# Experts, passes two and three: the second product by Strassen's scheme as well, with its operands turned round and a written-out order

## The chip, the cores and the metric

One core of a Trainium2 chip. The metric is the device time of one execution in microseconds (us): 1692.89 us is the median of three runs of the kernel before (1692.16 to 1692.99). The engines are PE (TensorE: matmuls; PEld is its loading of weights), DVE (VectorE), ACT (ScalarE), POOL (GpSimd) and SP, which here only issues DMA transfers.

## The reference, cut to what matters

Causal attention with decay gives `x`, 2304 tokens by 512. The mixture of experts then computes, with `P` a 2304 x 8 gate matrix made by eight rounds of row and column scaling:

```
for e in range(E):                      # E = 8
    h = np.maximum(x @ w1[e], 0.0)      # 512 -> 1024
    ye = h @ w2[e]                      # 1024 -> 512
    out += P[:, e:e + 1] * ye
```

The change is in this loop. The gate values are exponentials times positive scalings, so they are positive.

## The kernel before, in words

Attention runs first, in an order that a planner in the kernel (`arrange`) lays out from a table of durations; it fills the first 240 us or so. The experts follow in three passes of 768 tokens each (two halves of `HT` = 384). In a pass, a unit is one expert `e` and one block `fb` of 256 of its 1024 hidden features: 32 units in a pass, of which two of the first pass are done during attention. Every fp32 operand is split into a high part and a low part (`hi`, `lo`), and each matrix product is three matmuls: hi*hi, hi*lo, lo*hi.

The first product of a unit (`first_fast`, matmuls on L1201) uses Strassen's scheme: seven products of sums of quarter matrices in place of eight. A product is 6 matmuls of 384 columns, so a unit has 42. Its weight sums (S1 to S4) are formed and split in every pass anew, on POOL and ACT (`weight_sums`, `split_sums`); the token sums (T1 to T4) once per pass. DVE adds the seven products up (L1207), ACT and DVE make the high and low part of the relu (`hh` L857, `hl` L860).

The second product (`second`, `combine`, matmuls on L871) is plain: 6 tiles of 128 tokens, each 6 matmuls of 512 columns, 36 in a unit. DVE multiplies each result by the gate value and adds it to `acc` (L1249). A unit's second product stands on PE behind the first product of the unit after it. The last unit of a pass sends `acc` out.

In the expert part each engine works through its queue in the order of the code, except for SP, whose place for a transfer is decided by the framework; an SP transfer that waits holds back those behind it. Two buffers hold raw halves of w1 (`rw`), two of w2 (`rq`). A half is 256 KB.

## Time and profile before

| what | value |
|---|---|
| median of three runs | 1692.89 us |
| span of the profiled execution | 1696.4 us |
| PE busy in the span | 1689.7 us |
| DVE / POOL / ACT busy | 1335.6 / 1120.9 / 682.9 us |
| moved by DMA | 133.11 MB |
| granted TensorE clock, mean | 1.000 |

The profiled execution's own time is its span, 3.5 us above the median of the runs. Busy time of PE is from the start of a matmul to its modelled end; matmuls overlap, so what one costs is read from the distance between starts.

### The profile page before, as it was taken

What the parts mean: (1) busy time and instruction counts of PE and PEld (TensorE: products, weight loads), DVE (VectorE), ACT (ScalarE), POOL (GpSimd) and SP (SyncE); (2) the same over time, 40 slices, a digit from 0 to 9 for tenths busy, and PEclk for the clock granted to TensorE, in tenths of its full rate; (3) what the DMA queues carried; (4) which work ended last, traced back from release to release, by engine and by line L of the source; (5) the groups of instructions that cost most, each with busy time, mean ns of one, the idle gap of its engine ahead of it and who ended that gap; (6) DMA issues with size and microseconds to landing.
All of it is one profiled execution on the core that took longest, in us unless ns stands there. A gap on an engine that the chain in (4) does not pass through costs nothing. (4 is left out here: it accounts for less than half of the span.)

```text
span 1696.4 us, 26313 instructions
## 1 busy us (share of the span) xinstructions
PE 1689.7 (100%) x9179; PEld 1506.5 (89%) x9179; DVE 1335.6 (79%) x2273; ACT 682.9 (40%) x1445; POOL 1120.9 (66%) x1092
## 2 busy tenths in 40 slices
PE   9999999999999999999999999999999999999999
PEld 7888898989898998999899989998998999899988
DVE  6888869888778777777787788777777877787786
ACT  6877743433333333333333333333333333333332
POOL 4556375677766798766666666798766666666663
PEclk9999999999999999999999999999999999999999
DMA  5656312222222222322222222222322222222221
GB/s 133 162 143 161 96 53 69 69 64 74 69 67 65 69 72 63 109 69 69 62 75 70 69 63 69 75 62 63 112 70 64 73 69 69 63 74 71 69 63 62
DMA packets 147098, 133.11 MB, mean 78 GB/s; under 512 B 67371, under 2 KB 116886, under 8 KB 146966
## 3 DMA queue, kind: packets, MB, share of 16 engines
q1 hardware_dynamic: 146966, 131.44, 26.7%
q8 instruction: 72, 1.18, 0.3%
q14 instruction: 60, 0.49, 0.1%
HBM read 126.48 MB, written 4.92 MB: 77 GB/s over the span
## 5 line engine op out<-in xcount | busy, mean ns | idle before, releaser
L871 PE MATMUL po<-early_w,hh 128*128 128x512 f32 x2308 | 715.0, 391 | 1.8 <-DVE acc L1249 1.4
L871 PEld LDWEIGHTS po<-early_w,hh 128*128 128x128 f32 x2308 | 429.1, 188 | 90.2 <-DVE acc L1249 4.1
L1207 DVE TENSOR_TENSOR u<-ph,u 128x384 f32<-128x384 f32 x637 | 344.3, 553 | 205.2 <-PE ph L1201 196.1
L871 PE MATMUL po<-early_w,hl 128*128 128x512 f32 x1154 | 450.6, 391 | 0.0
L1146 POOL TENSOR_TENSOR early_w<-w,early_w 128x512 fp32r<-128x512 f32 x184 | 234.8, 1298 | 306.2 <-ACT early_w L1145 305.4
L860 DVE SCALAR_TENSOR_TENSOR hl<-u,hh 128x384 fp32r<-128x384 f32 x364 | 427.6, 1175 | 12.0 <-ACT hh L857 11.9
L1249 DVE SCALAR_TENSOR_TENSOR acc<-po,prob,acc 128x512 f32<-128x512 f32 x517 | 369.0, 741 | 80.8 <-PE po L871 80.8
L1145 ACT CAST early_w<-w 128x512 fp32r<-128x512 f32 x194 | 120.7, 622 | 553.7 <-issue 535.0
L857 ACT ACTIVATE hh<-u 128x384 fp32r<-128x384 f32 x364 | 190.0, 523 | 320.5 <-DVE u L1207 320.3
L1201 PE MATMUL ph<-t,early_w 128*128 128x384 f32 x1638 | 298.5, 334 | 0.0
L1167 POOL TENSOR_TENSOR early_w<-ws,early_w 128x1024 fp32r<-128x1024 f32 x91 | 222.4, 2444 | 110.4 <-ACT early_w L1164 109.3
L1201 PEld LDWEIGHTS ph<-t,early_w 128*128 128x128 f32 x1638 | 286.0, 188 | 0.0
L871 PEld LDWEIGHTS po<-early_w,hl 128*128 128x128 f32 x1154 | 216.6, 188 | 45.4
L1201 PE MATMUL ph<-xhi,wa 128*128 128x384 f32 x728 | 216.1, 337 | 0.0
L1168 POOL TENSOR_TENSOR wa<-w,wa 128x512 fp32r<-128x512 f32 x91 | 145.5, 1599 | 0.0
L1201 PEld LDWEIGHTS ph<-xhi,wa 128*128 128x128 f32 x728 | 134.1, 188 | 3.5
L1201 PE MATMUL ph<-xlo,wa 128*128 128x384 f32 x364 | 122.3, 336 | 0.0
L1201 PE MATMUL ph<-t,wa 128*128 128x384 f32 x546 | 109.3, 334 | 0.0
L1201 PE MATMUL ph<-xhi,early_w 128*128 128x384 f32 x364 | 107.0, 334 | 0.0
L1164 ACT CAST early_w<-ws 128x1024 fp32r<-128x1024 f32 x91 | 95.8, 1053 | 13.4 <-POOL ws L1157 9.6
L1201 PEld LDWEIGHTS ph<-t,wa 128*128 128x128 f32 x546 | 95.9, 188 | 0.0
L579 ACT ACTIVATE e<-e,mn 128x128 f32<-128x128 f32 (+3 forms) x128 | 70.6, 554 | 12.2 <-DVE mn L572 12.1
(149 smaller groups left out, 1844.8 us busy)
## 6 DMA issues: line engine op xcount, KB each, us to landing
w<-in_moe_w_dram SPq DMA_DIRECT2D x384, 256.0 KB
dn<-cum_d SPq DMA_DIRECT2D x14, 576.0 KB
out_dram<-acc SPq DMA_DIRECT2D x17, 256.0 KB
q<-in_q_dram SPq DMA_DIRECT2D x32, 128.0 KB
k<-in_k_dram SPq DMA_DIRECT2D x32, 128.0 KB
v<-in_v_dram SPq DMA_DIRECT2D x32, 128.0 KB
rb<-r SPq DMA_DIRECT2D x22, 128.0 KB
rz<-in_q_dram SPq DMA_DIRECT2D x32, 16.0 KB
```

The source lines that it names most:

```text
L579: nc.scalar.activation(out=t, in_=t, func=AF.Exp, scale=-1.0, bias=mn[at][:, 0:1], accum_out=place(ss, "ss")[:, at:at + 1],)
L857: nc.scalar.activation(out=hh[:, 0:w], in_=ph[:, 0:w], func=AF.Relu)
L860: nc.vector.scalar_tensor_tensor(out=hl[:, 0:w], in0=ph[:, 0:w], scalar=0.0, in1=hh[:, 0:w].bitcast(F32), op0=ALU.max, op1=ALU.subtract)
L871: nc.tensor.matmul(po[:, cols], ht[:, ts], wt[:, ft, cols], start=(ft == 0 and n == 0), stop=(ft == FB - 1 and n == 2))
L1145: nc.scalar.copy(out=hi[:, s], in_=r)
L1146: a = lo_on.tensor_tensor(out=lo[:, s], in0=r, in1=hi[:, s].bitcast(F32), op=ALU.subtract)
L1164: nc.scalar.copy(out=wsum[0], in_=t)
L1167: nc.gpsimd.tensor_tensor(out=wsum[1], in0=t, in1=wsum[0].bitcast(F32), op=ALU.subtract)
L1168: nc.gpsimd.tensor_tensor(out=lo[:, 1:3], in0=k1, in1=hi[:, 1:3].bitcast(F32), op=ALU.subtract)
L1201: nc.tensor.matmul(ps, ws[y][:, c], xs[z], start=(c == 0 and m == 0), stop=(c == KH - 1 and m == 2))
L1207: nc.vector.tensor_tensor(out=out, in0=in0, in1=in1, op=ALU.add)
L1249: nc.vector.scalar_tensor_tensor(out=to, in0=po[:, cols], scalar=prob[:, t, e:e + 1], in1=to, op0=ALU.mult, op1=ALU.add)
```

## The change

- **Pass one** stays, but each unit's seven weight combinations (high and low) are also written to DRAM (`keep_w1`), for the 27 units that have them there; the gate values of the other two passes are turned and stored (`spread_weights`).
- **Passes two and three** are new. Units are taken in pairs, (e, fb) and (e, fb+1). The seven products of the first scheme (`hidden_product`) read their weights from DRAM, 256 KB each; three of them add in place in one PSUM bank. The result is multiplied by the gate row in the same DVE instruction as the relu (`weigh_relu`), so that the second product can be summed over all experts.
- **The second product** (`out_product`) uses the same scheme, transposed: w2's seven combinations are stationary, the seven combinations of h move, 384 columns at a time. One accumulation takes both units of a pair: 6 matmuls. DVE adds it to one of seven sums M1 to M7 (L1761). Only at the end of a pass are the M's combined (`final_sums`, 7 additions of 768), turned back by PE transposes (`final_turn`) and stored.
- w2's sums and splits (`prepare_w2`), the splits of seven h operands in place of four, and the weight sums of the five units that pass one lacks (`prepare_w1`), with the token sums of pass three kept in DRAM (`prepare_x`), are new work for DVE, POOL and ACT.
- **Order:** the planner lays all this out. PE's order is fixed by the code: for a pair, the products 1, 7, 6, 2, 5, 3, 4 of both units, with the second products 1, 6, 7, 5, 3, 2, 4 of the pair before it between them. The planner's clocks start at PE 16, DVE 12, ACT 10, POOL 10, SP 2 us.

The core of the diff:

```diff
+    def keep_w1(e, fb):
+        d = w1_d[e, fb] = dram.tile([len(COMBOS), P, 2, KH * P], F32, name=f"w1d{e}{fb}")
+        for x in range(2):
+            for ts, a, z in ((wa, 0, 3), (wsum, 3, 7)):
+                nc.sync.dma_start(
+                    out=d[a:z, :, x].rearrange("s p f -> p s f"),
+                    in_=ts[x].rearrange("p s k f -> p s (k f)").bitcast(F32),
+                )
...
                 split_sums(r1, ws)
+                keep_w1(*work[m + 1][1:3])
...
     second(*late)
+    pctx.close()
...
+        "b": [banks[t] for t in ("M0", "M1", "A4", "A5", "A0", "A1")],
+        "s": [banks[t] for t in ("A2", "A3")],
+        "w": w_own + w_acc + from_h,
...
+        if which == "1":
+            keep("u1", X0, X, s)
+        elif which == "7":
+            keep("u7", X2, X, s)
+        elif which == "2":
+            op("c11", X1, X1, t["u1"], ALU.add, ["F2", "u1"], [X, bs["u1"]])
+            weigh_relu("H11", X1, X1, 0, [u.s["c11"]], [X])
+            split("H11", X1, [u.s["H11"]], [X], True)
+        elif which == "6":
+            new("u3")
+            op("u3", t["u3"], X0, t["u7"], ALU.add, ["F6", "u7"], [X, bs["u7"], bs["u3"]])
+        elif which == "5":
+            op("c22", X2, X0, t["u7"], ALU.add, ["F5", "u7"], [X, u.X[2], bs["u7"]])
...
+    moving = {"1": "H11", "3": "H22", "7": "T3", "5": "T1", "6": "T2", "2": "H21", "4": "T4"}
+
+    def out_product(us, which, M, begun, added):
...
+        for k in range(2):
+            b = Buffer("s")
...
+                for (h, _h), (w, _w) in zip(hs, ws):
+                    for y, z in ((0, 0), (0, 1), (1, 0)):
+                        nc.tensor.matmul(
+                            at_(b)[:, 0:HT], at_(w)[y][:, k * P:(k + 1) * P], at_(h)[:, z], start=(i == 0), stop=(i == 5)
+                        )
+                        i += 1
+            s = fpe(6 * pe(HT), run, after=[x for _, d in hs + ws for x in d], uses=[b] + [x for x, _ in hs + ws])
...
+                if begun:
+                    nc.vector.tensor_tensor(out=to, in0=at_(b)[:, 0:HT], in1=to, op=ALU.add)
+                else:
+                    nc.vector.tensor_copy(to, at_(b)[:, 0:HT])
...
+    arranged = arrange(fsteps, slots2, {"PE": 16.0, "DVE": 12.0, "ACT": 10.0, "POOL": 10.0, "SP": 2.0}, 250.0, True)
+    with tc.manual_schedule():
+        for s in arranged:
+            s.run(s.engine)
```

**Where pass one ends.** Before, SP has only the raw halves of w1 and w2 here, unit after unit:

```order
L842 DMA w<-in_moe_w_dram 128x2x256 x2
L842 DMA w<-in_moe_w_dram 128x512 x2
L842 DMA w<-in_moe_w_dram 128x2x256 x2
L842 DMA w<-in_moe_w_dram 128x512 x2
```

Now SP has, from the last stores of `acc` that a pass makes, the first eight weight combinations (`wn`), the gate rows (`pb`) and only then the first raw halves of w2 (`w_8854`, `w_8855`):

```order
L1261 DMA out_0_dram<-acc4_85 128x512
L1626 DMA wn0_8811<-w1d70_8109 128x512
L1261 DMA out_0_dram<-acc5_86 128x512
L1626 DMA wn1_8812<-w1d71_8261 128x512
L1626 DMA wn_8838<-w1d70_8109 128x512
L1626 DMA wn_8839<-w1d71_8261 128x512
L1626 DMA wn_8830<-w1d70_8109 128x512
L1626 DMA wn_8831<-w1d71_8261 128x512
L1626 DMA wn_8832<-w1d70_8109 128x512
L1626 DMA wn_8833<-w1d71_8261 128x512
L1616 DMA pb_8822<-p_d_89 128x768
L850 DMA w_8854<-in_moe_w2_dram 128x512
```

The first load of a combination, `wn0`, goes into memory that the last second product of pass one reads. Behind it, ACT's queue stands like this (L1674 copies product 1 of a unit, from bank M0 and then M1, out of PSUM):

```order
L1156 CAST early_w10_110<-w_8621 128x512
L1448 CAST w2n0_8813<-w_8854 128x256
L1674 COPY u_8850<-bankM0_8842 128x384
L1448 CAST w2n1_8814<-fourw_8841 128x256
L1674 COPY u_8851<-bankM1_8843 128x384
```

The copy of product 1 stands behind the cast of a raw half of w2, and that of the second unit behind a sum of both halves (`fourw`). PE's fifth and sixth products add into M0 and M1 and need these copies.

**In the middle of a pass.** Before, DVE's queue for a unit reads:

```order
L1207 TENSOR_TENSOR u<-ph,u 128x384 x5
L860 SCALAR_TENSOR_TENSOR hl_4249<-u,hh_4248 128x384
L1207 TENSOR_TENSOR u<-ph,u 128x384
L860 SCALAR_TENSOR_TENSOR hl<-u,hh 128x384
L1207 TENSOR_TENSOR u<-ph,u 128x384
L860 SCALAR_TENSOR_TENSOR hl_4245<-u,hh_4244 128x384
L1249 SCALAR_TENSOR_TENSOR acc_83<-po,prob,acc_83 128x512
```

Now it reads, in pass three, behind product 3 of a pair's two units (in banks A0 and A1):

```order
L1679 SCALAR_TENSOR_TENSOR tn_8837<-bankA0_8846,pb_8822 128x384
L1459 TENSOR_TENSOR tn_8834<-tn_8837,bankM0_8842 128x384
L1679 SCALAR_TENSOR_TENSOR u_8853<-bankA1_8847,pb_8822 128x384
L1459 TENSOR_TENSOR u_8852<-bankA4_8844,tn_8834 128x384
L1459 TENSOR_TENSOR u_8851<-u_8853,bankM1_8843 128x384
L1761 TENSOR_TENSOR sum3_8826<-bankA3_8849,sum3_8826 128x384
L1459 TENSOR_TENSOR tn_8835<-bankA5_8845,u_8851 128x384
L1761 TENSOR_TENSOR sum3_8826<-bankA2_8848,sum3_8826 128x384
L1459 TENSOR_TENSOR tn_8834<-bankA4_8844,tn_8837 128x384
```

Nearly every row has one operand in PSUM (`bank`); there are 48 rows for a pair.

**Where pass two's result is turned back, and at the end.** PE's queue at the end of the program (L1752 are second products, L1790 transposes), where there was nothing but the plain second product of the last unit before:

```order
L1790 MATMUL bankA3_8849<-ident_75,sum2_8825 128x128 x2
L1790 MATMUL bankA3_8849<-ident_75,sum4_8827 128x128 x2
L1790 MATMUL bankA2_8848<-ident_75,sum2_8825 128x128 x2
L1790 MATMUL bankA2_8848<-ident_75,sum4_8827 128x128 x2
L1752 MATMUL bankA2_8848<-xlo_80,w2n3_8816 128x384 x3
L1752 MATMUL bankA2_8848<-xhi_79,early_w20_112 128x384 x2
L1752 MATMUL bankA2_8848<-xhi_79,early_w21_113 128x384
L1752 MATMUL bankA2_8848<-xlo_80,w2n3_8816 128x384 x3
L1790 MATMUL bankA3_8849<-ident_75,sum1_8824 128x128 x2
L1790 MATMUL bankA2_8848<-ident_75,sum3_8826 128x128 x2
```

Transposes and second products share the two banks A2 and A3, and the last second product has both its halves in A2.

## Rows read from the trace of the kernel before

**Rows 1.** The page: busy time, share of the span, number of instructions.

```profile
PE 1689.7 (100%) x9179; PEld 1506.5 (89%) x9179; DVE 1335.6 (79%) x2273; ACT 682.9 (40%) x1445; POOL 1120.9 (66%) x1092
```

**Rows 2.** Stretches: PE, PEld, DVE, ACT, POOL busy; clock, DMA share, GB/s.

```profile
0.00:240.00 240.00, 238.41 (x1888) 194.14 (x1889) 187.34 (x626) 169.22 (x501) 126.77 (x209) 1.00 0.50 130
560.00:1660.00 1100.00, 1099.75 (x5530) 996.21 (x5530) 862.54 (x1205) 388.53 (x715) 768.09 (x687) 1.00 0.24 71
```

**Rows 3.** PE in order of time, one unit: start, length.

```profile
1404.76 0.33 PE L1201 MATMUL ph<-xhi,wa 128*128 128x384 f32 x1
...
1412.06 0.63 PE L871 MATMUL po<-early_w,hh 128*128 128x512 f32 x2
...
1420.26 0.33 PE L1201 MATMUL ph<-xhi,wa 128*128 128x384 f32 x1
```

**Rows 4.** DVE, one unit in order of time.

```profile
1409.14 1.60 DVE L1207 TENSOR_TENSOR u<-ph,u 128x384 f32<-128x384 f32 x3 [0.48 <-PE ph L1201]
...
1411.98 0.54 DVE L860 SCALAR_TENSOR_TENSOR hl<-u,hh 128x384 fp32r<-128x384 f32 x1
...
1412.91 2.29 DVE L860 SCALAR_TENSOR_TENSOR hl<-u,hh 128x384 fp32r<-128x384 f32 x1
```

**Rows 5.** POOL in the same unit.

```profile
1412.34 2.45 POOL L1167 TENSOR_TENSOR early_w<-ws,early_w 128x1024 fp32r<-128x1024 f32 x1 [1.17 <-ACT early_w L1164]
```

**Rows 6.** Groups from 1000 to 1660 us: count, busy us, mean ns.

```profile
L1207 DVE TENSOR_TENSOR u<-ph,u 128x384 f32<-128x384 f32 x300 | 162.3, 553 | 100.2 <-PE ph L1201 98.2 <-ACT u L1211 1.3
L1154 POOL TENSOR_TENSOR ws<-w 128x256 f32<-128x256 f32 x43 | 31.7, 738 | 0.0
L1112 POOL TENSOR_TENSOR ts<-xhi,ts 128x384 f32<-128x384 f32 x2 | 2.0, 1020 | 0.2
L857 ACT ACTIVATE hh<-u 128x384 fp32r<-128x384 f32 x170 | 88.8, 523 | 153.8 <-DVE u L1207 153.8
L1145 ACT CAST early_w<-w 128x512 fp32r<-128x512 f32 x86 | 53.5, 622 | 262.5 <-issue 260.0
L1211 ACT COPY u<-ph 128x384 f32<-128x384 f32 x43 | 20.3, 473 | 0.0
L1163 ACT CAST wa<-w 128x256 fp32r<-128x256 f32 x43 | 17.5, 407 | 11.2 <-PE ph L1201 11.2
```

**Rows 7.** POOL in pass one, in order of time.

```profile
483.12 1.60 POOL L1168 TENSOR_TENSOR wa<-w,wa 128x512 fp32r<-128x512 f32 x1
...
492.10 0.74 POOL L1155 TENSOR_TENSOR ws<-w 128x256 f32<-128x256 f32 x1
...
498.62 1.62 POOL L1168 TENSOR_TENSOR wa<-w,wa 128x512 fp32r<-128x512 f32 x1
```

**Rows 8.** Stretches in which one half of w1, released at 484.7, arrives.

```profile
484.50:485.50 1.00, 1.00 (x6) 0.81 (x6) 1.00 (x2) 0.00 (x0) 0.23 (x1) 1.00 0.00 0
485.50:486.50 1.00, 1.00 (x6) 0.84 (x5) 1.00 (x3) 0.00 (x0) 0.00 (x0) 1.00 0.55 119
486.50:487.50 1.00, 1.00 (x7) 0.81 (x5) 0.65 (x2) 0.00 (x0) 0.00 (x0) 1.00 0.42 143
```

**Rows 9.** DMA from 1198 to 1208, GB/s in 40 slices of 0.25 us.

```profile
GB/s 0 0 0 0 0 0 0 0 0 94 98 205 242 369 418 377 328 402 401 410 401 393 410 401 402 402 369 164 8 0 16 106 90 98 213 360 402 401 352 287
```

**Rows 10.** PE where pass two begins, and PE and DVE at the end.

```profile
690.83 0.33 PE L1201 MATMUL ph<-xhi,wa 128*128 128x384 f32 x1
...
706.34 0.33 PE L1201 MATMUL ph<-xhi,wa 128*128 128x384 f32 x1
...
1692.12 0.51 PE L871 MATMUL po<-early_w,hh 128*128 128x256 f32 x2 [0.58 <-DVE acc L1249]
...
1693.14 0.48 DVE L1249 SCALAR_TENSOR_TENSOR acc<-po,prob,acc 128x256 f32<-128x256 f32 x1 [1.07 <-PE po L871]
```

**Rows 11.** PE transposes in the attention part.

```profile
200.24 0.49 PE L715 MATMUL pt<-ident,e 128*128 128x128 f32 x3
```

More of the change, by code (lines that the diff above doesn't have):

```diff
@@ L1305, in attention_then_moe @@
         hts = hts_of[m % 2]
-        if m + 1 < len(work) and work[m + 1][4]:
+        if not last and fast_next:
             ws = weight_sums(r1)
@@ new lines, in loads, with psum_op, lock_op, eng @@
+    def loads(kb, run, line, **kw):
+        s = fstep({"SP": 0.07}, run, behind=[in_turn[line]] if line in in_turn else [], lands=DMA_LANDS, kb=kb, **kw)
+        in_turn[line] = s
+        return s
+    def psum_op(w=HT): return 0.1 + w / 960
+    def lock_op(w): return {"POOL": 0.1 + w / 400, "DVE": 0.14 + w / 960}
+    def eng(e):
+        return nc.gpsimd if e == "POOL" else nc.vector
+    def hi_step(src, dst, w, after, uses, behind=(), due=None):
+        def run(_):
+            nc.scalar.copy(out=dst(0), in_=src())
+        return fstep({"ACT": 0.19 + w / 1200}, run, after=after, uses=uses, behind=list(behind), due=due)
@@ new lines, in final_sums, with add, run @@
+    def final_sums(M, added):
+        last, chain = {}, []
+        def add(i, j):
+            def run(en):
+                eng(en).tensor_tensor(out=at_(M[i - 1]), in0=at_(M[i - 1]), in1=at_(M[j - 1]), op=ALU.add)
+            after = [x for y in (i, j) for x in last.get(y, added[y - 1, 0] + added[y - 1, 1])]
+            s = fstep({"DVE": 0.09 + 2 * HT / 960}, run, after=[*after, *chain[-1:]], uses=[M[i - 1], M[j - 1]], lock=True,
+                      due=(added[max(i, j, key=lambda y: backs.index(str(y))) - 1, 1][0].due[0], 1.2))
+            chain.append(s)
+            last[i] = [s]
+        return last, add
```

510 lines of the change are left out of this document (467 added, 43 removed).

## Prediction

> **What bounds the kernel now.** I read the page's line of busy times first: PE is busy for 1689.7 of 1696.4 us, the next engine, DVE, for 1335.6 [rows 1]. The stretches say that this holds everywhere: 1099.75 of 1100 us in the experts, 238.41 of 240 in the attention part, and the granted clock is 1.00 in both, which is the 2.4 GHz level [rows 2]. So time is gained only where PE gets fewer columns, and every gap that opens on PE costs its full length. Then I read PE in order of time over one unit, to get prices as distances between starts, not as busy time: the first product takes 1412.06 - 1404.76 = 7.30 us for 42 matmuls of 384 columns, 0.1738 each; the second 1420.26 - 1412.06 = 8.20 us for 36 matmuls of 512 [rows 3]. A unit is 15.50 us. Last I read PE at both ends of the changed part. Pass two starts at 690.83, its second unit 15.51 later [rows 10]. The last second product of pass one follows the first 7.30 us of pass two, so in the new program, which puts it ahead, the new passes start at 690.83 + 8.20 = 699.03. From there 64 units at 15.506 (the mean of those two periods) are 992.4 and reach 1691.5. The span's end is 4.9 later.
>
> **The gain on PE.** A second product becomes seven products of two tiles of 128 rows, each 3 matmuls of 384 columns for a unit: 42 matmuls in place of 36 of 512. At 0.1738 that is 7.30 us in place of 8.20. 64 units by 0.90 are **-57.6 us**. The first product keeps its count. A pair of units at full pace takes 4 x 7.30 = 29.2 us; before, 31.0. Everything below asks whether the other engines keep up with 29.2, and what the four edges cost.
>
> **Can DVE hold 29.2?** I count 48 rows in DVE's queue for a pair: 44 of 384 columns with an operand in PSUM, 4 with both in SBUF. The nearest row is L1207, 553 ns each [rows 6]; three in a row take 1.60, so they start 0.50 to 0.53 apart [rows 4]. 44 at 0.50 to 0.553 and 4 at 0.54 are 24.2 to 26.5 us, 83 to 91% of the pair. That fits, if the SBUF rows stay at 0.54. They need not: the same `hl` row took 0.54 at 1411.98 and 2.29 at 1412.91 [rows 4], and the second lies under a POOL row of 2.45 us that began at 1412.34 [rows 5]. Four such delays of 1.75 us are 7.0: 31.2 to 33.5 in the worst case, nothing in the best. POOL's rows in the new part are short (0.738 and 1.02 [rows 6]), so a delay can't be longer than those: I take 1 us for half of the four, 2 us a pair, which still leaves DVE under 29.2.
>
> What the Trainium skill says bears on this ("SBUF — State Buffer", section "Who interferes with whom"): VectorE with two SBUF inputs contends with a GpSimd instruction that reads SBUF, and with at most one SBUF input it doesn't. By it the 44 rows are safe and only four are at risk. The two `hl` rows agree with it; no row here shows the new forms under a busy POOL.
>
> **POOL and ACT.** POOL gets 8 rows of 384 columns (1.02) and 18 of 256 (0.738 [rows 6]) in a steady pair: 21.4 us. In pass two the sums for the five missing units and for pass three's tokens bring it to about 28. ACT has some 32 copies and casts of 0.407 to 0.523 [rows 6]: 15 us. Both are hidden under PE. The longest chain in a pair is from the end of product 3 to the second product that reads its T's: relu row, three DVE sums, a cast on ACT (0.52), a low part on POOL (1.02), with DVE's other rows between them, some 6.2 us against 8 products of PE, 8.3. The slack is about 2 us, and some pairs will lose it. For this, and for POOL in pass two, I put **+4** (bounds 0 and 15: half a microsecond in each of 32 pairs is 15).
>
> **Transfers.** A pair loads 14 combinations and 4 raw halves of 256 KB and its part of the gate rows, 4.9 MB, 168 GB/s at 29.2. DMA has shown 400 GB/s in a stretch [rows 9]. The loads are asked for a pair ahead, so nothing on PE. In pass one, 27 units write 1.83 MB more each, 118 GB/s on top of 71 [rows 2]. What could hurt there is SP's order: the second raw half of w1 is queued behind the writes. It was released at 484.72 and its last bytes came by 487.4 [rows 7, 8]; POOL first uses it at 492.10 and the split that PE needs is done near 498.6 [rows 7], with the next unit's need near 505. Some 7 us are free, 1.83 MB take 4.6 at 400 GB/s. **0** in pass one (bound +10, if every third unit misses by 1). `spread_weights` is one more set of short rows: **+1**.
>
> **The end of pass one.** Before, the next unit's weights lay ready. Now `wn0` goes into memory that the last second product reads, so it is released by the last matmul. A half of 256 KB took 2.7 us from release to the last byte: 1.0 to the first, 1.7 of transfer [rows 8]. So PE waits about 3. Loads three and on wait for the stores of `acc4` and `acc5`. The fifth product adds into M0 and needs ACT's copy of product 1, which is queued behind the cast of `w_8854`, and this load stands behind eight combinations and the gate rows: 2.75 MB at 400 GB/s are 6.9, plus 3, plus cast and copy (0.41 and 0.47): at +10.8 instead of 3.0 + 4 x 1.04 = 7.2. A second wait of 3.6. Then DVE has w2's sums in front of the first unit's sums; I allow 2.4. **+9** (6 if the copies run early, 13 if both stores come late).
>
> **Turning back after pass two.** Seven sums of 768 columns on DVE (two times 0.54 each, 7.6 us, in a pair in which DVE has 26), and 24 transposes of 0.11 on PE [rows 11], 2.6 us. Transposes and second products share A2 and A3, and each of the six changes of bank waits for a copy out, some 0.9. **+8** (4 to 12).
>
> **The end.** Behind the last second product's place: the 12 transposes ahead of it 1.3; its second half waits for DVE in the same bank 1.1; then an add (0.55), a sum of 768 (1.1) and the wake-ups, 2.2; transposes and two drains of a bank 2.0; a copy 0.5; a store 2.8, as the 256 KB above. That is 9.9 past the plain pace, where before it was 4.9, an add of 0.48 at 1693.14 and a store [rows 10]. **+5** (3 to 8).
>
> **Sum.** -57.6 + 9 + 8 + 5 + 4 + 1 = -30.6. The profiled span 1696.4 becomes 1665.8; the median of the runs lies 3.5 below its span, so **1662**.
>
> **Rivals.**
> - *The edges cost little*: 6, 4 and 3 in place of 9, 8 and 5, no friction: -43.6, **1649**. For it: a layout by the same planner kept PE at 238.41 of 240 in the attention part, far less regular work [rows 2]. Against it: the released-late load is in the order itself. 0.14.
> - *The clock falls.* In the stretches shown the clock is 1.00 and PE never waits long; the new program has waits of 3 us at two or three edges. If PE comes back at 1.2 GHz, the first group of 14 products, 14.6 us, at worst takes twice as long; I take 3 us at each of two edges, +6, **1668**. No row here shows the lower level, so 0.13. The skill has such a rule ("TensorE: Matmul & The Clock Gate", section "HAM oscillation — how this bites in real kernels"): waits between groups of matmuls put the clock back to half. No run shown here tests it.
> - *DVE becomes the bound, slower than before.* The gain less the edges (57.6 - 27) over 32 pairs is 0.96: at 30.16 us a pair nothing is left. With 48 rows that is a mean of 0.628 each, against 0.50 to 0.553. DVE waits behind POOL at each of the four SBUF rows, or wake-ups between rows that alternate banks, would do it: at 30.0 a pair +26, **1688**; at 0.65 a row (31.2) +64, **1726**. For it: 0.48 and 1.07 of wait stand before DVE rows even now [rows 4, 10], and the queue is in a fixed order. Against it: those waits are for PE. 0.10, of which 0.07 slower.
> - *Transfers pace it.* SP's queue is in order; were its 18.7 loads of a pair to go one by one at 1.7 us [rows 8], a pair takes 31.8, +83, **1745**. Against it: 400 GB/s with several in flight [rows 9]. 0.05, mostly mild cases that leave some gain; 0.02 slower.
> - The forecast has the remaining 0.58, from 1653 to 1675 by its own bounds.
>
> **Numbers.** A change of under 0.2% (3.4 us) is about what a measurement of this kernel can't tell from none. Faster 0.88, the same 0.03, slower 0.09. From 1649 to 1684 leaves out half of the first rival, most of DVE's and the transfers': 0.2.
>
> **What the profile after would show.** Right: PE rows of a pair 29.2 apart in passes two and three; no gap inside a pair over 0.5; at the end of pass one a gap of 3, ended by a load of `wn0`, then one of 3 to 4 ended by ACT's copy; DVE at 80 to 90% in the two passes; transposes (L1790) waiting for ACT or DVE copies. Wrong: a period above 29.7 with waits for DVE sums (rival three) or for `wn` loads (four); units in pass one above 15.55; a granted clock under 1.00 after an edge.

## The result, and the profile after

The changed kernel takes 1680.24 us (median; 1678.60 to 1681.46), the kernel before 1692.94 beside it: 12.7 us less. The ratio on record, from all these runs, is 0.9911 with a 95% interval of 0.9893 to 0.993 (the two medians alone give 0.9925). The prediction was 1662, 30.6 us less. The sign was right, the size was not: some 18 us of the expected gain did not come.

The page of the changed kernel begins with busy time, share of the span (1677.4) and instructions, as [rows 1] did before:

```profile
PE 1646.8 (98%) x9617; PEld 1545.4 (92%) x9617; DVE 1377.6 (82%) x2781; ACT 772.3 (46%) x1882; POOL 1158.8 (69%) x1360
```

PE now idles 30.6 us in all (6.7 before). Its stretches show where (columns as in [rows 2]):

```profile
700.00:760.00 60.00, 52.67 (x268) 51.26 (x268) 41.15 (x82) 23.75 (x61) 36.06 (x46) 0.89 0.77 234
...
1200.00:1300.00 100.00, 93.94 (x536) 92.47 (x535) 79.04 (x158) 44.62 (x108) 67.13 (x83) 0.98 0.54 166
1300.00:1400.00 100.00, 100.00 (x579) 100.00 (x578) 81.44 (x165) 46.21 (x112) 73.04 (x89) 1.00 0.57 170
```

Pass three (1300 on) is what the prediction wanted: PE full, DVE at 81%, DMA at 170 GB/s. The losses lie at 700 to 760, around 1000 (PE is busy for 97.92 of the 100 us from 900), around 1210, at the end, and in one place of pass one, 545 to 583. PE's list of waits names who ended them:

```profile
PE bankA L1752 <- DVE sum L1763: 5.3, 3, 3.9
PE bankM L1660 <- DMA wn<-w1d: 4.1, 2, 3.0
PE bankM L1660 <- ACT u L1674: 3.2, 2, 2.4
PE bankA L1752 <- POOL early_w L1453: 2.8, 6, 0.7
```

These four make 15.4 of the 30.6 us. But the losses that are added up below come to 46.3 us, and PE idles only 23.9 more than before. So about half of them is a slower clock and added work, which one sees only in distances between starts. PE in pass three, first matmuls of product 1 in different pairs:

```profile
1304.25 0.33 PE L1660 MATMUL bankM<-xhi,wn 128*128 128x384 f32 x1
...
1362.49 0.33 PE L1660 MATMUL bankM<-xhi,wn 128*128 128x384 f32 x1
```

They are two pairs apart: 58.24, that is 29.12 a pair (29.2 forecast), 14.56 a unit. PE where pass one ends:

```profile
699.62 0.39 PE L879 MATMUL po<-early_w,hl 128*128 128x512 f32 x1
702.98 0.41 PE L1660 MATMUL bankM<-xhi,wn 128*128 128x384 f32 x1 [2.97 <-DMA wn<-w1d]
...
713.75 1.75 PE L1660 MATMUL bankM<-t,wn 128*128 128x384 f32 x6 [2.41 <-ACT u L1674]
716.32 2.29 PE L1660 MATMUL bankM<-t,wn 128*128 128x384 f32 x6 [0.82 <-ACT u L1674]
...
728.30 0.69 PE L1752 MATMUL bankA<-xhi,w2n 128*128 128x384 f32 x3
```

The last matmul of pass one ends its turn at 699.85 (0.23 after its start). The first second product comes at 728.30, 28.45 later, where the 14 products between need 14.56: a loss of 13.9. Both waits of the forecast are there (3.0 for the first load and 1.1 for the second, 2.4 and 0.8 for ACT's copy), and something it gave 13 in 100: matmuls 0.32 apart. The stretches of 2 us show the clock (the column behind the engines):

```profile
702.00:704.00 2.00, 1.02 (x6) 0.99 (x6) 0.00 (x0) 0.00 (x0) 0.00 (x0) 1.00 0.70 229
704.00:706.00 2.00, 0.88 (x4) 0.61 (x3) 0.00 (x0) 0.00 (x0) 0.00 (x0) 0.54 0.84 291
708.00:710.00 2.00, 2.00 (x7) 2.00 (x7) 0.00 (x0) 0.00 (x0) 0.00 (x0) 0.50 0.88 291
712.00:714.00 2.00, 0.25 (x1) 0.25 (x2) 0.41 (x1) 0.78 (x2) 1.12 (x2) 1.00 1.07 384
716.00:718.00 2.00, 1.68 (x5) 1.68 (x6) 0.83 (x3) 2.00 (x7) 1.74 (x3) 0.50 0.73 197
722.00:724.00 2.00, 2.00 (x13) 2.00 (x12) 1.97 (x4) 1.03 (x3) 0.00 (x0) 1.00 0.87 250
```

After the wait of 3 us PE's granted clock is 1.00 at 702, then 0.54 and 0.50 (1.2 GHz) at 704 to 710. From 712 to 714, where PE does almost nothing, it reads 1.00; behind that wait it is at 0.50 once more, and at 722 it is 1.00 again. Of the 13.9 us PE idles 7.3; the rest is the slow pace.

To add up, one needs a start that both kernels share, since executions of the same kernel differ by some us in their first 20 us (last section). The same unit of pass one begins at 457.62 in the profile before and at 452.86 after:

```profile
457.62 0.33 PE L1201 MATMUL ph<-xhi,wa 128*128 128x384 f32 x1
```

```profile
452.86 0.34 PE L1212 MATMUL ph<-xhi,wa 128*128 128x384 f32 x1
```

From there to the end of the span: 1696.4 - 457.62 = 1238.8 before, 1677.4 - 452.86 = 1224.5 after. (The second profile of the kernel before gives the same 1238.8: 1694.3 - 455.54.) The change is worth **-14.2 us** on that basis, and its terms are (us):

| term | forecast | measured | from |
|---|---|---|---|
| second product, 64 units | -57.6 | -60.5 | 15.506 - 14.56 a unit |
| end of pass one | +9 | +13.9 | 28.45 - 14.56 |
| turning back after pass two | +8 | +12.2 | a step of 33.01 (1196.35 to 1229.36) where 20.80 is plain |
| the end | +5 | +6.3 | last plain product due at 1666.17, end 1677.4: 11.2 past, 4.9 before |
| friction in pass two | +4 | +8.2 | 447.09 from 728.30 to pass three's first product, plain 438.88 |
| pass one | +1 | +5.7 | three units 52.19 long in place of 46.52 |
| sum | -30.6 | -14.2 | |

"Plain" is a stretch without any loss: its matmuls at 0.1733 each. The rows for friction and for turning back (pass three's first product, then the two ends of the step, which is five sevenths of a pair) are:

```profile
1175.39 0.33 PE L1660 MATMUL bankM<-xhi,wn 128*128 128x384 f32 x1
...
1196.35 0.33 PE L1660 MATMUL bankM<-xhi,wn 128*128 128x384 f32 x1
...
1229.36 0.34 PE L1660 MATMUL bankM<-xhi,wn 128*128 128x384 f32 x1
```

The term of pass one lies in this stretch of PE (starts of three units, and a wait):

```profile
544.61 0.34 PE L1212 MATMUL ph<-xhi,wa 128*128 128x384 f32 x1
...
565.37 0.33 PE L1212 MATMUL ph<-xhi,wa 128*128 128x384 f32 x1
...
579.53 0.72 PE L879 MATMUL po<-early_w,hh 128*128 128x512 f32 x2 [1.22 <-DVE acc L1257]
...
582.58 0.33 PE L1212 MATMUL ph<-xhi,wa 128*128 128x384 f32 x1
```

One unit takes 20.76, the next 17.21; the one ahead of them takes 14.22, since part of its second product fell behind it, so the three are 52.19 long. It is where `spread_weights` turns the gate values: its 12 transposes run from 537.7 to 547.6. PE idles 2.5 us there (0.23, 0.46, 0.59 and 1.22, ended by DVE's `acc` and POOL's low parts). No run leaves `spread_weights` out, so the cause is put down to it by the place alone. The other units of pass one take 15.51, as before, so the writes of `keep_w1` cost nothing, as forecast.

### The profile page after: what moved, and what is told of

The parts are those of the page before. It is cut to its first block, busy times and chain, and to the rows that moved or that the text cites. A ratio compares the mean times of both kernels' runs of the same rounds, so it can differ in the third digit from the quotient of the medians.

```text
span 1677.4 us, 29706 instructions
## 1 busy us (share of the span) xinstructions
PE 1646.8 (98%) x9617; PEld 1545.4 (92%) x9617; DVE 1377.6 (82%) x2781; ACT 772.3 (46%) x1882; POOL 1158.8 (69%) x1360
## 4 chain that ended last, share of the span: by engine, by line
PE 50%; DVE 3%; DMA 3%; POOL 2%; issue 1%; ACT 1%; SPq 0%; DVEq 0%; POOLq 0%; ACTq 0%
PE bankA L1752 24%; PE bankA L1660 14%; PE bankM L1660 10%; DMA w<-in_moe_w_dram 1%; PE po L879 1%; DMA w1d<-four 1%; DVE sum L1761 1%; PE ph L1212 0%; DVE sum L1772 0%; POOL early_w L1453 0%; POOL fourw L1590 0%; POOL four L1453 0%; POOL w2n L1453 0%; DVE bankA L1459 0%; DVE bankA L1679 0%
## 5 line engine op out<-in xcount | busy, mean ns | idle before, releaser
L1761 DVE TENSOR_TENSOR sum<-bankA,sum 128x384 f32<-128x384 f32 x420 | 231.9, 553 | 76.3 <-PE bankA L1752 73.2
L879 PE MATMUL po<-early_w,hh 128*128 128x512 f32 x768 | 241.8, 395 | 4.5 <-DVE acc L1257 2.3
L1660 PE MATMUL bankA<-t,wn 128*128 128x384 f32 x960 | 181.7, 337 | 0.0
L879 PEld LDWEIGHTS po<-early_w,hh 128*128 128x128 f32 x768 | 141.0, 188 | 36.6 <-DVE acc L1257 5.2
L1660 PEld LDWEIGHTS bankA<-t,wn 128*128 128x128 f32 x960 | 170.3, 190 | 0.0
L879 PE MATMUL po<-early_w,hl 128*128 128x512 f32 x384 | 150.3, 391 | 0.0
L1218 DVE TENSOR_TENSOR u<-ph,u 128x384 f32<-128x384 f32 x189 | 102.0, 552 | 57.0 <-PE ph L1212 48.5
L1752 PE MATMUL bankA<-xhi,early_w 128*128 128x384 f32 x606 | 135.2, 335 | 1.6 <-POOL early_w L1453 1.6
L868 DVE SCALAR_TENSOR_TENSOR hl<-u,hh 128x384 fp32r<-128x384 f32 x108 | 126.0, 1167 | 13.1 <-ACT hh L865 12.8
L1752 PE MATMUL bankA<-xlo,early_w 128*128 128x384 f32 x528 | 118.9, 335 | 2.3 <-POOL early_w L1453 1.2
L1257 DVE SCALAR_TENSOR_TENSOR acc<-po,prob,acc 128x512 f32<-128x512 f32 x144 | 102.4, 741 | 21.1 <-PE po L879 20.9
L1157 POOL TENSOR_TENSOR early_w<-w,early_w 128x512 fp32r<-128x512 f32 x56 | 71.6, 1302 | 64.5 <-ACT early_w L1156 63.6
L1752 PEld LDWEIGHTS bankA<-xhi,early_w 128*128 128x128 f32 x606 | 107.5, 188 | 3.5 <-POOL early_w L1453 2.8
L1752 PE MATMUL bankA<-xhi,w2n 128*128 128x384 f32 x480 | 109.9, 335 | 0.7 <-POOL w2n L1453 0.4
L1752 PE MATMUL bankA<-xlo,w2n 128*128 128x384 f32 x474 | 108.8, 337 | 1.4 <-DVE sum L1761 0.7
```

What stands on the lines that cost most here:

```text
L868: nc.vector.scalar_tensor_tensor(out=hl[:, 0:w], in0=ph[:, 0:w], scalar=0.0, in1=hh[:, 0:w].bitcast(F32), op0=ALU.max, op1=ALU.subtract)
L879: nc.tensor.matmul(po[:, cols], ht[:, ts], wt[:, ft, cols], start=(ft == 0 and n == 0), stop=(ft == FB - 1 and n == 2))
L1157: a = lo_on.tensor_tensor(out=lo[:, s], in0=r, in1=hi[:, s].bitcast(F32), op=ALU.subtract)
L1218: nc.vector.tensor_tensor(out=out, in0=in0, in1=in1, op=ALU.add)
L1257: nc.vector.scalar_tensor_tensor(out=to, in0=po, scalar=prob[:, t, e:e + 1], in1=to, op0=ALU.mult, op1=ALU.add)
L1660: nc.tensor.matmul(ps, wt[:, y, c * P:(c + 1) * P], x[z], start=(start and c == 0 and m == 0), stop=(c == KH - 1 and m == 2), skip_group_c ...
```

## The experiments

Seventeen kernels beside one more run of the kernel before, read by three distances, since they are free of the first 20 us. *Boundary*: from the last matmul of pass one to the first second product (plain 14.6). *Friction*: from there to pass three, above 438.9. *Change*: the step of five sevenths of a pair across the turning back (plain 20.8). The times are medians, or one run where the kernel computes something else.

| run | boundary | friction | change | us |
|---|---|---|---|---|
| the change | 28.5 | 8.2 | 33.0 | 1680.24 |
| warm | 28.0 | 6.2 | 33.9 | 1681.75 |
| early_loads | 25.0 | 8.0 | 33.4 | 1679.24 |
| early_all | 24.1 | 7.4 | 33.4 | 1679.52 |
| copies_first | 22.9 | 10.1 | 33.3 | 1678.98 |
| first_clear | 23.1 | 9.5 | 33.5 | 1678.59 |
| sums_pool | 28.6 | 9.0 | 34.9 | 1681.57 |
| sums_first | 28.8 | 8.7 | 27.9 | 1676.93 |
| writes_on_act | 28.7 | 8.9 | 33.5 | 1683.91 |
| no_chores | 27.8 | 0.1 | 28.6 | 1672.90 |
| no_store | 27.6 | 0.1 | 27.6 | 1669.53 |
| no_compute | 27.6 | 4.2 | 33.2 | 1678.12 |
| small_writes | 27.9 | 8.3 | 33.6 | 1683.63 |
| no_w1_load | 26.7 | 7.7 | 33.2 | 1676.94 |
| combined | 19.5 | 10.7 | 27.9 | 1678.08 |
| combined2 | 18.1 | 20.6 | 27.9 | 1676.23 |
| combined2_rate | 17.9 | 34.1 | 29.7 | 1698.02 |
| combined5 | 17.7 | 8.7 | 27.1 | 1669.50 |

(The expectations speak of 8.4 us of friction, counted from pair to pair.) What comes ahead of the end of pass one is in none of the three distances. So here is the whole from the shared start to the end of the span, for some: the change 1224.5 us, warm 1223.4, early_loads 1221.8, early_all 1222.5, copies_first 1221.2, sums_first 1220.6, combined 1220.8, combined2 1222.5, combined5 1209.6.

**The base.** The kernel before, once more.

> The kernel before, unchanged, profiled once more. The sum of the prediction was made against a profiled span of 1696.4 us, 3.5 above the median of the runs, while the changed kernel's profiled execution has a span 1.8 below its own time. Theory: the first profiled execution was an unusually long one by about 5 us, so half of the missing gain (about 6 of 18 us) is an error of the base: a second profile then has a span near 1691. Rival: the profile of this kernel is always longer; then the span is again near 1696.

Its span is 1694.3 at a time of 1696.12, so a span is 1.8 below its own time (not equal to it, as the table of the time before has it), and the first profile's 1696.4 was an execution about 5 us longer than the median. Neither expectation is met well. This does not touch the forecast of the difference, but it makes the two spans (19.0 apart) flatter the change by about 5 us.

**The edge where pass one ends: clock or waits?**

```diff
+            for _i in range(idle):
+                nc.tensor.matmul(banks["A3"][:, 0:HT], x_hi[:, 0, 0:P], x_hi[:, 1, 0:HT], start=True, stop=True)
```

> PE gets 48 matmuls whose result nobody reads (14, 5, 26 and 3 ahead of the first, second, fifth and sixth product of pass two), to fill the four waits where pass one ends. After the change matmuls start 0.32 apart from 705.4 to 721.3 there, in place of 0.174. Theory 1 (the waits let the clock fall): the granted clock stays at 1.00, the fifth product still starts at about 713.7 (it waits for ACT's copy behind the load of w2), and the first second product of the pass comes about 3.3 us earlier than 28.6 us after the last matmul of pass one: -3 us in all. Theory 2 (the clock falls for another reason, say the new work itself): it falls all the same, and the time is the same or longer.

The same stretches of warm:

```profile
708.00:710.00 2.00, 1.66 (x10) 1.34 (x9) 0.00 (x0) 0.00 (x0) 0.00 (x0) 1.00 0.84 272
716.00:718.00 2.00, 1.31 (x8) 0.99 (x6) 0.00 (x0) 0.42 (x2) 0.45 (x1) 1.00 1.05 384
```

The clock stays at 1.00: the idle time let it fall. But the boundary is only 0.5 us shorter (28.0), not 3.3. PE reached its next waits sooner and waited there (0.7 us for ACT's copy, 0.6 for DVE ahead of product 3). So the slow clock was real and mostly filled time in which PE had nothing to do. It is one execution, and its fifth product came 0.8 us later than in the change (14.7 us after pass one, 13.9 there), so the clock may be worth up to 1.3 us here. What sets most of this edge is loads and queues.

```diff
-        "w": w_own + w_acc + from_h,
+        "w": from_h + w_own + w_acc,
...
+    for n, (fb, name) in enumerate(((0, "A11"), (1, "A11"), (0, "S3"), (1, "S3"))):
+        nc.sync.dma_start(out=from_h[n].bitcast(F32), in_=w1_d[E - 1, fb][COMBOS.index(name)])
     second(*late)
```

> The first four weight combinations of pass two go to four buffers that are free a unit earlier, and their loads are issued ahead of the last unit of pass one. Theory (PE waits for loads released by the last matmul): the first wait of 2.97 and the second of 1.12 us are gone; the fifth product still waits for ACT's copy behind the cast of w2, but that load now has four fewer ahead of it (2.6 us at 400 GB/s), so it starts near 711 in place of 713.7; with the clock up behind it, the pass is 5 to 6 us earlier. Rival (only the queue behind w2 counts): PE waits there for the whole time, and no more than 3 us come back.

> As early_loads, and the two raw halves of w2 of the first unit are also loaded ahead, into buffers that are free. Theory: nothing of the 13.7 us lost where pass one ends is left but 1 to 2 us, the granted clock stays at 1.00 there: -12 us, about 1668. Rival: the first group of products is bound by DVE, ACT and POOL work in front of it (w2's sums and casts), so 4 us or more of the 13.7 remain.

early_loads: the fifth product starts 11.7 us after pass one (13.9 in the change) and PE waits 7.35 for ACT's copy; 3.4 us come back, between the two expectations. In early_all the fifth product comes at 5.7 and ACT's copy holds nothing, but PE then waits 2.6 for a load of `wn` and 1.4 for DVE, and 24.1 is all that is reached. Besides, DVE's queue got w2's sums ahead of pass one's last sums into `acc`, and stood for the load, so that pass one ended 2.4 us later than in early_loads:

```profile
697.58 0.42 DVE L1602 TENSOR_TENSOR fourw<-w 128x256 f32<-128x256 f32 x1 [5.51 <-DMA w<-in_moe_w_dram]
697.92 0.74 DVE L1257 SCALAR_TENSOR_TENSOR acc<-po,prob,acc 128x512 f32<-128x512 f32 x1
```

An earlier load had moved a row forward, and the row stood for it ahead of others.

```diff
-            a = hi_step(src, dst, H2, after, [*uses, b], behind=[line] if line else [])
+            a = hi_step(src, dst, H2, after, [*uses, b], behind=[line] if line else [*copies])
```

> The early loads of before (four combinations ahead of the end of pass one), and in ACT's queue the first pair's copies of products 1 and 7 stand ahead of the casts of w2. Counted from the last matmul of pass one, the fifth product started at 13.9 us in the change, 11.7 with early loads alone, and the first second product at 28.5 and 25.0. Theory (ACT's queue held PE): the fifth product starts at 4.2 to 6, and the granted clock holds for the first eight products; what is left is the transfer of 10 more combinations and 4 halves of w2 at some 290 GB/s, 12 to 14 us: the first second product comes at 17 to 20, -8 to -11 us for the change as it was. Rival (the first group is bound by its transfers whatever the order): it stays at 23 or more.

```diff
-            made[o] = fstep(lock_op(H2), run, after=got + [made[x] for x in needs], uses=[v[o], *uses], lock=True,
+            made[o] = fstep({"POOL": 0.74} if first else lock_op(H2), run, after=got + [made[x] for x in needs], uses=[v[o], *uses], lock=True,
```

> The early loads and ACT's order of the runs before, and now also DVE's queue is cleared where pass two begins: w2's sums and low parts of the first unit are POOL's alone, and the first extra weight sums stand behind the first pair's sums. With ACT's order alone PE waited 5.0 us for DVE, whose queue stood at w2's sums until w2 landed, 10.9 us after the last matmul of pass one; the first second product came at 22.9 us. Theory (DVE's queue held PE there): that wait is under 1 us, the clock does not fall in the first 14 products, which end at 15 to 16 us; then PE waits for the second unit's w2, whose loads stand behind the first unit's splits, and the first second product comes at 18 to 21. Rival (transfers hold everything): 22 or more.

With ACT's copies first the fifth product comes at 4.2, and PE waits 5.0 us for DVE in place of ACT (w2's sums again). With DVE cleared too, it waits 5.0 us for a load of `wn`: the two halves of raw w1 for the first extra sums stood ahead of it on SP. The rival's number came (23.1), but its reason, that transfers hold everything whatever the order, did not hold: with another order on SP the edge came down to 18.1 (combined2, below). Four holds in a row kept the same edge.

**Turning back.** In the change DVE does this ahead of the wait of 3.9 us (start, length):

```profile
1207.98 1.01 DVE L1453 TENSOR_TENSOR xhi<-bankM,xhi 128x384 fp32r<-128x384 f32 x2
1208.90 0.55 DVE L1459 TENSOR_TENSOR tn<-bankM,tn 128x384 f32<-128x384 f32 x1
1209.37 1.33 DVE L1772 TENSOR_TENSOR sum<-sum,sum 128x768 f32<-128x768 f32 x1
1210.74 1.02 DVE L1763 COPY sum<-bankA 128x384 f32<-128x384 f32 x2
```

L1763 puts a product into M1, which the sixth sum (L1772) still reads. In DVE's queue that sum stands 25 rows behind the fifth. Behind the wait the granted clock is 0.59 (1212 to 1216).

```diff
-            s = fstep({"DVE": 0.09 + 2 * HT / 960}, run, after=[*after, *chain[-1:]], uses=[M[i - 1], M[j - 1]], lock=True,
+            s = fstep(on, run, after=[*after, *chain[-1:]], uses=[M[i - 1], M[j - 1]], lock=True,
...
-        last, add = final_sums(p.M, p.added)
+        last, add = final_sums(p.M, p.added, ("DVE", "POOL"))
```

sums_first, the second kernel below, instead makes the sums due 8 us ahead of M's last part, where they were due 1.2 behind it:

> The seven sums of 768 between pass two and pass three may go to POOL as well; the planner puts two on DVE and five on POOL. In the change the step from one pair to the next takes 33.0 us at this place in place of 20.8, and PE waits 3.9 us there for a copy on DVE (L1763) that stands behind such sums. Theory 1 (DVE has more work in this pair than it has time): with five sums gone the wait is under 1 us, the clock stays up, and the step takes 27 to 29: -4 to -6 us. Theory 2 (the chain of sums itself is what the copy waits for, as the copy overwrites a sum that the chain still reads): POOL's sums of 768 at some 2 us each make the chain longer, the wait grows to 6 us or more, and the step is 35 or longer.

```diff
-        last, add = final_sums(p.M, p.added)
+        last, add = final_sums(p.M, p.added, -8.0)
```

> The sums of 768 between pass two and three stay on DVE, but the planner ranks them as due 9 us earlier, so that the sixth (M2 += M1) stands two rows behind the fifth in DVE's queue and not 25 rows behind it. PE waits 3.9 us for the copy that puts the first second product of pass three into M1 (L1763), and this copy may only come when the sixth sum has read M1. Without the extra work of pass two, where the planner happened to put the sixth sum early, the step from pair to pair here was 28.6 us in place of 33.0. Theory (the place of one sum in DVE's order sets this wait): the step is 28 to 30 us, the clock stays at 1.00 behind it: -3 to -5 us. Rival (the extra work itself delays the pass change, through POOL or transfers): 32 us or more.

sums_pool fits neither expectation: PE waits 1.6 and 3.5 us there for w2's parts, which now stand behind POOL's sums (34.9). sums_first is met: the long wait is gone, the clock stays up, 27.9. The place of these sums in DVE's queue was worth 5 us; how much of that is the wait of 3.9 and how much the clock is not separated.

**Friction in pass two.** PE waits for low parts of w2. POOL at that place:

```profile
958.13 0.74 POOL L1548 TENSOR_TENSOR four<-w 128x256 f32<-128x256 f32 x1 [4.13 <-DMA w<-in_moe_w_dram]
```

First the writes through ACT's queue, then no extra work at all:

```diff
-                nc.sync.dma_start(out=where(x), in_=at_(o[x])[:, 0:w])
+                nc.scalar.dma_start(out=where(x), in_=at_(o[x])[:, 0:w])
...
-                    nc.sync.dma_start(out=d[i, :, x].rearrange("p (k f) -> p k f", f=P), in_=at_(o)[x])
+                    nc.scalar.dma_start(out=d[i, :, x].rearrange("p (k f) -> p k f", f=P), in_=at_(o)[x])
```

> The writes of the weight sums and token sums that pass two makes for itself (5 units and 2 parts) go to ACT's DMA queue in place of SP's. In pass two PE loses 8.4 us against the plain pace, from 955 us on, mostly to low parts of w2 on POOL, while POOL itself waits for raw halves of w2; SP's queue is held by such writes for 12.2 us of 950 to 1070, and the loads stand behind them. Theory 1 (SP's order makes the raw halves late): at most 3 of the 8.4 us are left, -5 us. Theory 2 (POOL has too much work in these pairs): the 8.4 us stay.

```diff
-    chores = [lambda q=q: prepare_w1(*q) for q in order_of if q in lacking] + chores
+    chores = []
+    for q in lacking:
+        w1_d[q] = w1_d[E - 1, q[1]]
```

> The weight sums of the five units that pass one lacks and the token sums of pass three aren't made: other units' combinations and pass two's token sums are read in their place. All three theories on pass two's 8.4 us (SP's queue, POOL's work, DMA traffic) expect the loss to be gone, under 1 us, so that every pair takes 29.1; if 4 us or more stay, the loss has nothing to do with this extra work, and lies in the pairs themselves.

Then its parts: the work without the writes (no_store), the writes without the work (no_compute, where the eight sums over x, the four over w1 and the low parts are left out), an eighth of the bytes of the weight sums (the 16 writes of token sums stay whole), and no load of raw w1.

```diff
-            done.append(fstep({"SP": 0.07}, run, after=[s], uses=[o[x]], lands=DMA_LANDS, kb=w / 2))
+            done.append(s)
...
-                done[name].append(fstep({"SP": 0.07}, run, after=[s], uses=[o, *v], lands=DMA_LANDS, kb=w / 2))
+                done[name].append(s)
```

> The extra work of pass two is computed as in the change (sums, casts, low parts, loads of raw w1) but not written to DRAM; later pairs read other units' combinations, and pass three the token sums of pass two. Pass two lost 8.4 us against 29.12 a pair in the change, 0 without the extra work. Theory 1 (POOL's and DVE's time): 5 us or more of the 8.4 stay. Theory 2 (DMA traffic: these writes go in packets of 512 bytes, 128 KB each, beside 220 GB/s): under 3 us stay.

```diff
-        z = lo_step(src, dst, w, [a], [*uses, *o])
-        for x, s in ((0, a), (1, z)):
+        for x, s in ((0, a), (1, a)):
```

> The counterpart: the raw loads, the casts on ACT and all writes of the extra work stay, its sums and low parts on POOL and DVE are left out, and the casts' results are written twice. Theory 1 (POOL's and DVE's time): under 3 us of the 8.4 stay. Theory 2 (DMA traffic): 5 us or more stay.

```diff
-                    nc.sync.dma_start(out=d[i, :, x].rearrange("p (k f) -> p k f", f=P), in_=at_(o)[x])
+                    nc.sync.dma_start(out=d[i, 0:16, x].rearrange("p (k f) -> p k f", f=P), in_=at_(o)[x][0:16])
```

> The change, with all instructions and their order kept, but each of the 70 writes of pass two's extra weight sums carries 16 of 128 partitions, an eighth of the bytes; later pairs read other units' combinations in place of these five. Pass two lost 8.4 us in the change, none when the writes were left out of the plan, and 8.6 when they went through another queue. Theory A (the transfers themselves take DMA time from the loads): under 2.5 us stay. Theory B (what counts is the plan with such writes, that is the order and the buffers that it gives, not their transfer): 6 us or more stay.

```diff
-                if rs[n].tile is None:
-                    rs[n].tile = load_half(e, fb, "w1", n, at_(rs[n]))
+                rs[n].tile = x_hi[:, n, 4 * HT:4 * HT + HALF].bitcast(F32).rearrange("p (c f) -> p c f", f=FB * P)
```

> The change, with the same order on every engine but SP, which does not load the raw w1 of the five units; their sums and casts read tokens of x that lie in memory, so they never wait for a transfer, and all later work and writes stay. Pass two lost 8.4 us in the change, where POOL stood 4.1 us at 958 for a raw half of w1 while w2's low parts, which PE then waits for, were queued behind. Theory P (POOL, in order, stands at the extra rows until raw w1 lands): under 3 us of the 8.4 stay. Rival (w2's own halves are late, or the order is too tight without any load): 6 us or more stay.

All friction comes from the extra work (no_chores 0.1). It isn't its work on POOL and DVE alone: no_store keeps that work and has none. It isn't the bytes written: an eighth of them in the same order leaves 8.3. It isn't SP's queue (8.9 through ACT's) nor POOL's wait for raw w1 (7.7). no_compute, with the writes and without the sums, keeps 4.2, between the bounds of its two theories (under 3, 5 or more). What no_store lacks besides bytes is that a buffer is held until a write lands, and it gets another order from the planner, as no_chores and no_compute do. So neither the bytes nor engine time alone is the cause, and the plan with held buffers is left. The lists of waits agree with that: from 725 to 1178 us POOL, ACT and DVE wait 13.3 us in the change for writes of extra work to land, and 10.6 in small_writes, with an eighth of the bytes. The chain of the change, followed back from 1010 us, has such a write ahead of each of two stalls of PE (start, length; the stalls end at 963.28 and 994.84):

```profile
950.79 3.68 DMA x_d<-w
...
986.57 3.58 DMA w1d<-four
```

Ahead of the first stall a load of raw weights (5.5 us) and three sums on POOL also stand in that chain, so this is a sign, and no proof.

**Together.** combined has the loads of w1 and w2 ahead, copies first, w2's first sums on POOL, the first extra weight sums behind the first pair, and the sums of the turning back moved up; the next three add to it.

> All that helped, in one: four combinations and the first unit's raw w2 are loaded ahead of the end of pass one, ACT's copies stand first, w2's first work is POOL's, the first extra weight sums come behind the first pair, and the sums between the passes are ranked early. Theory: the first second product comes 17 to 20 us after pass one (28.5 in the change), the pass change takes 28 (33.0), pass two's friction stays near 8: -13 to -16 us against the change, 1664 to 1668 beside a before of 1693 to 1696. Rival (the boundary is bound by its transfers): it comes at 23 or later, and the sum is -9 to -11.

```diff
-    chores = [lambda c=c: prepare_x(c) for c in range(KH)]
+    chores = [lambda c=c: prepare_x(c, pair_done) for c in range(KH)]
```

> As combined, and the token sums of pass three may begin only when the pair ahead of them is done, so that they no longer stand ahead of pass one's last sums into acc on DVE (which cost 5.0 us of PE's time in combined, and let the clock fall). The boundary was 19.5 us from the last matmul of pass one to the first second product there, and the pass change 27.9. Expected: no wait of over 1 us ahead of the last matmul of pass one, boundary 18 to 20, pass change 28, friction near 8: 13 to 15 us below the change at the same begin of pass one, 1664 to 1668 in the median.

```diff
-    arranged = arrange(fsteps, slots2, {"PE": 16.0, "DVE": 12.0, "ACT": 10.0, "POOL": 10.0, "SP": 2.0}, 250.0, True)
+    arranged = arrange(fsteps, slots2, {"PE": 16.0, "DVE": 12.0, "ACT": 10.0, "POOL": 10.0, "SP": 2.0}, 200.0, True)
```

> As combined2, but the planner reckons with 200 GB/s of DMA in place of 250 (pass two shows 200 to 230 in the pairs with extra work), and the sums between the passes may lie beside POOL's rows. Theory (the plan is too early for the transfers, so rows stand ahead of others whose data is there): pass two's friction falls from 8 to under 5, the rest as combined2: 1661 to 1665. Rival (it depends on single rows, not on the rate): the friction stays at 6 to 12.

> The mended edges of combined2 (boundary 18.1 us, pass change 27.9), with the token sums of pass three allowed from the end of the first pair on, in place of one pair late (which had put them behind weight sums that waited for writes to land: one stall of 15.7 us at 1081), and with three separate buffers of 1 KB per partition for the high and low parts on their way to DRAM, in place of one of 2 KB that holds both. Theory L (the extra rows wait for the writes of the rows before them to land, and w2's parts stand behind them on POOL and ACT in order): with a third buffer the friction of pass two falls below 5 us, and the median is 1661 to 1664. Rival (the order is tight in any case): friction 7 or more, or a single stall; with 8 us the median is 1665.

(combined2_rate and combined5 also let the sums between the passes lie beside POOL's rows.) In combined5 the token sums begin once, not pair by pair, and each half of a w1 sum has a buffer of its own:

```diff
-    chores = [lambda c=c: prepare_x(c, pair_done) for c in range(KH)]
+    chores = [lambda c=c: prepare_x(c, x_begins) for c in range(KH)]
...
-        "c": [[four[:, 0:2, 2 * P:3 * P], four[:, 2:4, 2 * P:3 * P]]],
+        "c": [four[:, 0:2, 2 * P:3 * P], four[:, 2:4, 2 * P:3 * P], c_own],
```

combined gains at its boundary and gives the gain back ahead of it: token sums moved before pass one's last rows, PE waits 5.0 us there, the clock falls (0.50 from 700 to 704), and pass one ends 7.7 us later than in the change. combined2 takes those away and gets one stall of 10.5 us at 1081. POOL, ACT and PE there:

```profile
1060.80 2.00 POOL L1503 TENSOR_TENSOR four<-xhi,xlo 128x384 f32<-128x384 f32 x2 [3.16 <-DMA w1d<-four]
```

```profile
1080.53 0.51 ACT L1456 CAST w<-four 128x384 fp32r<-128x384 f32 x1 [2.67 <-DVE w L1461]
1080.95 0.40 ACT L1456 CAST early_w<-w 128x256 fp32r<-128x256 f32 x1
```

```profile
1081.40 1.01 PE L1769 MATMUL bankA<-xlo,early_w 128*128 128x384 f32 x2 [10.50 <-ACT early_w L1456]
```

The first of eight token sums on POOL waits 3.2 us for a write to land. ACT's casts of these sums then wait 2.9 and 2.7 us for DVE's low parts of the sums before them, one of which had waited 0.7 us for a write of token sums to land. The cast of w2 that PE needs stands behind these casts in ACT's queue. combined2_rate's slower plan is worse (34.1): it loses 4.5 to 7.3 us at each of four places. combined5 keeps all edges: 1669.5 (1664.78 to 1673.37), a ratio to before of 0.9845 with an interval of 0.983 to 0.9861, the best here. From the shared start it is 29.2 us below the kernel before (1238.8), close to the forecast's 30.6, but by another order at the edges. PE in combined5:

```profile
711.47 2.32 PE L1678 MATMUL bankM<-t,wn 128*128 128x384 f32 x12 [1.52 <-DVE bankA L1697]
...
718.03 0.69 PE L1770 MATMUL bankA<-xhi,w2n 128*128 128x384 f32 x3
```

No wait over 1.6 us is left at the boundary, and its stretches show a clock of 1.00 from 700 to 720. Its friction is no smaller (8.7 where under 5 was expected), but it lies elsewhere: 1.5 us come by 751, the ten pairs behind that have none, and the other 7.2 come from 1067 on. So the third buffer did not prove the theory of held buffers.

## Why the prediction was wrong

- **What bounds the kernel, and the gain**: right. PE in pass three is full, and a unit takes 14.56 us (14.6 forecast); the gain was a little larger than the term.
- **DVE, transfers as the bound**: right that neither bounds a pair (DVE 81%, 170 GB/s). The rival of four contended DVE rows changed nothing here: pass three, with the same rows, has no friction. What the Trainium skill says there ("SBUF — State Buffer", section "Who interferes with whom") agrees with the trace: from 1310 to 1650 us, 514 DVE rows of 384 columns with an operand in PSUM took 0.55 us on the mean, under a POOL row or not (0.54 to 0.57), while 53 of 256 columns with both operands in SBUF took 0.41 beside an idle POOL and 0.41 to 0.99 under a POOL row. That is some 0.4 us a pair, where the forecast allowed 2.
- **The end of pass one**: the step named the right waits in the right order, and mis-sized the sum: 13.9 for 9, above its bound of 13. It priced three waits on one path. In truth the edge was held four times over, by the loads' release, ACT's queue, DVE's queue and SP's order; taking one away showed the next (28.5, 25.0, 22.9, 23.1, 18.1). Beside the waits stood 6.6 us of slow pace, which the sum did not have.
- **The rival of the clock**: its mechanism happened, and warm shows the cause (idle PE). Its price did not come: with the clock held at 1.00 the boundary was 0.5 us shorter (1.3 at most), where 3 were taken for this edge. At the other edge its price was not measured by itself. The Trainium skill ("TensorE: Matmul & The Clock Gate", section "HAM oscillation — how this bites in real kernels") agrees that idle time before a group slows it; here the slower group mostly stood in for a wait.
- **Turning back**: mis-sized, 12.2 for 8. Its 8 are the transposes (2.6) and six waits of 0.9, for which no row stood; of the seven sums it counted only the time on DVE. What cost was their place in the queue; moved up, the term is 7.1 (27.9 - 20.8), near the forecast, with waits of 0.3 to 0.7 at the changes of bank.
- **Friction**: +4 taken, 8.2 measured, inside the bounds. The first reason given (slack in the pair) was wrong: pairs without the extra work run at 29.12. The second (POOL's load in pass two) named the right work, but that work alone costs nothing (no_store 0.1). What stays open is by which wait the plan with it does so; order, held buffers and landing times were not told apart.
- **Pass one**: the writes cost nothing, as forecast. `spread_weights`, called one more set of short rows, stands where 5.7 were lost: the step that failed most in proportion. It puts 12 transposes between PE's rows and changes the order around them; PE's idle time is 2.5 of the 5.7, and no run took either away.
- **The end**: 6.3 for 5, right.

The step that failed is thus the sum of the losses beside the steady pairs, its terms +9, +8, +5, +4 and +1. Each was priced by its own rows and waits, without what the queues hold in front of it, and came out short, by 1.3 to 4.9 us: 19.3 in all (4.9 + 4.2 + 1.3 + 4.2 + 4.7), of which the larger gain gave 2.9 back. The 16.4 left are what is missing between -30.6 and -14.2 (the medians show 12.7 less). For the end of pass one and the turning back the runs show the cause; for friction and pass one it stays open as said.

## What to carry to other kernels

Here the steady loop was forecast from distances between starts to 0.3% (29.2 for 29.12 a pair); the error sat at the edges, where each engine's queue, in order, held the same product. So price an edge by going through every queue in front of it, and expect that mending one shows the next. A row added to a fixed order costs by what is queued behind it while it waits, not by its own length.

## What the runs showed that was not expected

- A few waits of 1 to 3 us in a row cost PE its clock at the end of pass one (0.50 at 708 and at 716, 1.00 from 722). Holding it at 1.00 was expected to give 3.3 us back, and the boundary became 0.5 shorter.
- Executions of one kernel differ in their first 20 us. The rows of 12 to 16 us, of the kernel before in its first profile and then in before_again:

```profile
12.00:16.00 4.00, 4.00 (x18) 2.84 (x20) 0.42 (x2) 1.09 (x4) 1.44 (x4) 1.00 0.36 82
```

```profile
12.00:16.00 4.00, 4.00 (x25) 3.26 (x24) 1.87 (x9) 1.70 (x6) 1.20 (x3) 0.50 0.36 82
```

In the second the clock is at 1.2 GHz, and yet it starts the experts 2.7 us earlier: the first second product comes at 218.93, and at 221.64 in the first profile (215.94 in the changed kernel, with a clock of 1.00 in these rows). So the clock is not what makes the difference; what does stays open. The steps are about those by which the times of the kernel before differ (1692.9, 1696.1, 1699.6). From the shared start on the two profiles agree (1238.8 both), and distances inside the trace see differences of under 1 us that a median of four runs does not.
